# Gate tiles copied to SBUF before the tanh, up tiles multiplied by the copy, first uses of buffers that no longer wait for each other, and longer assumed latencies, in a fused attention and SwiGLU block

## The chip, the cores and the metric

The kernel runs on one core of a Trainium2 chip. The metric is device microseconds (us) of one execution, lower is better. Quoted times are medians of a kernel's runs; ratios are always against runs of the kernel before on the same chip. A span, read from a profile, is about 2 us shorter than the timed run.

Engines in the profile: PE is TensorE (matmuls), PEld its weight loads, DVE is VectorE, ACT is ScalarE, POOL is GpSimd, SPq is the queue that issues the DMA transfers.

## The reference, cut to what matters

Shapes: S = 2048 rows, D = 1024, H = 32 heads of 32, one shared key and value head, F = 3584.

```python
h = layernorm(x) * (1 + ca) + sa              # sa ... gb from silu(c) @ w_mod
x = x + ga * attention(h, wq, wk, wv, wo)     # softmax over 2048 keys, 32 query heads, 1 kv head
h = layernorm(x) * (1 + cb) + sb
x = x + gb * ((silu(h @ w1) * (h @ w3)) @ w2)
```

The 2048 rows are worked off in 8 blocks of 256: attention of a block, then output projection, layer norm and feed-forward of that block. Feed-forward is 672 matmuls of 128x128 by 256 columns a block, 5376 in all.

## The kernel before

All instructions are collected in a graph. A list scheduler then puts them, when the program is built, into one fixed order for each engine, with assumed durations and latencies. The built program holds a list for each engine, with semaphore waits where the graph demands them; in the profile of the kernel before, for one, the weight loads of the scores waited 180.5 us for exps. So an instruction's place is decided by the assumptions, and its time is what the profile shows.

```python
SEM_LAT = 0.06                                   # assumed semaphore latency, us
class Dag:
    def add(self, eng, fn, reads=(), writes=(), dur=0.1, lat=0.1, prio=5, ...):
        ...
        for k in reads:                          # a read waits for the last writer of the key
            ...
        for k in writes:                         # a write waits for the last writer and all readers,
            ...                                  # and becomes the last writer
    def schedule(self, banks):                   # greedy: next free engine takes its best ready node;
        ...                                      # a PSUM bank is free once all nodes of its group ended
def dve_t(n, rate=1):
    return n / rate / 960.0 + 0.08               # assumed time of a VectorE operation
```

The program uses eight PSUM banks: six (SP) belong to the attention scores as long as there are any, two (PB) serve everything else. The feed-forward loop, for a pair of gate and up tiles (128 x 512 each):

```python
for fp in range(NF // 2):                        # 14 pairs a block
    sl, rk = ring()                              # weight slot; rk: keys that the slot lies over
    for w, src in enumerate((w1_in, w3_in)):
        dma(..., ("ring", sl, w), writes=[("RW", sl, w)] + (rk if w == 0 else rk[1:]), ...)
    for w in range(2):
        g = mm_group(2 * NC, gmm, ...)           # 16 matmuls into one PSUM bank
        if w == 0:
            G.add("act", lambda e, g=g: e.activation(TS[:, 0:2 * qn], PB[g.bank][:, 0:2 * qn], ACT.Tanh, scale=0.5),
                  writes=["TS"] + alias("TS"), groups=[(g, "r")], ...)
            G.add("dve", lambda e, g=g: e.scalar_tensor_tensor(          # (tanh + 1) * gate
                TT[:, 0:2 * qn], TS[:, 0:2 * qn], 1.0, PB[g.bank][:, 0:2 * qn], ALU.add, ALU.mult),
                reads=["TS"], writes=["TT"] + alias("TT"), groups=[(g, "r")], ...)
        else:
            G.add("dve", lambda e, g=g, fp=fp: e.tensor_tensor(HHT[...], TT[...], PB[g.bank][...], ALU.mult),
                reads=["TT"], writes=[("HHT", 2 * fp), ("HHT", 2 * fp + 1)] + alias(("HHT", fp)), ...)
```

`ring()` and `alias()` give, at the first use of a buffer, the keys of the older data under it. They are booked as writes, so each first use waits for the first use before it. At every use, first or not, `ring()` also gives a key RING of the slot, so that the first of a slot's two loads waits for the readers of both halves.

The softmax here doesn't subtract the row's maximum and nothing guards it: scores larger than these inputs give would overflow.

## Time and profile before

1299.79 us, median of 3 runs (1299.6 to 1301.11).

| stage of the profile (span 1298.3 us) | length | TensorE busy | VectorE busy | ScalarE busy |
|---|---|---|---|---|
| 100 us to the last score matmul at 1049.5 us | 949.5 us | 861 | 794 | 928 |
| from there to the end (the tail) | 248.8 us | 242 | 95 | 28 |

First the page of the kernel before: busy time by engine, and the span in 40 slices, busy share in tenths.

```profile
PE 1169.6 (90%) x15761; PEld 764.7 (59%) x15809; DVE 968.8 (75%) x1363; ACT 1009.1 (78%) x1146; POOL 28.5 (2%) x51
...
PE   4688987789899889997999979999799999999998
...
DVE  7788889868987888789887888878988865244242
ACT  1499999999999999999999989999999941011010
```

ScalarE is at 9 until slice 32 and then nearly idle, TensorE goes on to the end: two stages, with different limits. The whole-span shares hide this. The tail is feed-forward work that did not fit under attention.

The windows by stretch, kernel before: start:end, length, then busy us and count of PE, PEld, DVE, ACT, POOL, granted clock, DMA share, GB/s.

```profile
100.00:1049.50 949.50, 861.35 (x12604) 517.43 (x12635) 794.18 (x1058) 928.19 (x1043) 17.30 (x24) 0.96 0.46 129
1049.50:1298.30 248.80, 241.83 (x2205) 210.12 (x2201) 95.41 (x159) 27.62 (x45) 3.15 (x8) 1.00 0.99 264
```

The waits from 100 to 1050 us, kernel before: who waited for whom, us in total, times, longest.

```profile
PEld SP L702 <- ACT UREG L712: 180.5, 443, 2.2
...
ACT UREG L712 <- PE PB L655: 10.6, 6, 2.9
ACT UREG L712 <- PE SP L702: 9.9, 13, 1.5
```

L702 are the score matmuls, L712 the exps, L655 the value matmuls. TensorE waits for exps (180.5 us); ScalarE, busy 928 of the 949.5 us, hardly waits (10.6 and 9.9 us). ScalarE sets the pace here. (A weight load of the scores can wait while TensorE still multiplies: TensorE was idle for 88 of the 949.5 us in all.)

Groups by line and shape, kernel before: count, then busy us and mean ns of one, then idle before.

```profile
L830 ACT ACTIVATE WREG<-PB 128x512 bf16<-128x512 f32 x84 | 60.6, 722 | 70.3 <-PE PB L824 70.3
L833 DVE SCALAR_TENSOR_TENSOR WREG<-WREG,PB 128x512 bf16<-128x512 bf16 x84 | 56.8, 676 | 28.8 <-ACT WREG L830 25.8
...
L837 DVE TENSOR_TENSOR HREG<-WREG,PB 128x512 bf16<-128x512 bf16 x77 | 52.1, 676 | 9.8 <-PE PB L824 9.2
...
L866 DVE TENSOR_TENSOR X<-X,WREG 128x512 bf16<-128x512 bf16 x32 | 13.2, 413 | 0.7
```

A tanh out of PSUM (0.722 us) and two VectorE operations of 0.676 us each make a pair's product; L866 shows what a two-operand operation took when all was bf16 in SBUF (0.413 us).

### The profile page before, as it was taken

The numbers are of one execution on the slowest core, as the hardware profiler recorded it, in microseconds if no ns is written. First come the engines' busy times: TensorE is split into PE (matmuls) and PEld (weight loads), VectorE is DVE, ScalarE is ACT, GpSimd is POOL, SyncE is SP. The second block draws the span as 40 slices with busy tenths as digits, with TensorE's granted clock in tenths as the row PEclk, the third lists the DMA queues.
The fourth block names the chain that finished last, engine by engine and source line by source line (L and its number), as shares of the span: only waits on it lengthen the run. The fifth ranks groups of instructions, "written<-read, shape, count | busy, mean of one in ns | idle before, by whom it ended". The sixth has DMA issues, their size and how long they took to land.

```text
span 1298.3 us, 35924 instructions
## 1 busy us (share of the span) xinstructions
PE 1169.6 (90%) x15761; PEld 764.7 (59%) x15809; DVE 968.8 (75%) x1363; ACT 1009.1 (78%) x1146; POOL 28.5 (2%) x51
## 2 busy tenths in 40 slices
PE   4688987789899889997999979999799999999998
PEld 3333333455466446663666646665466678878887
DVE  7788889868987888789887888878988865244242
ACT  1499999999999999999999989999999941011010
POOL 1000000000100000000000000000100000000000
PEclk9898998989999989998999989999899999999999
DMA  9533001645256325571465724557155589999997
GB/s 311 197 104 110 2 2 34 178 134 139 76 162 196 99 69 165 158 205 57 133 175 152 218 76 132 147 166 210 34 164 147 162 245 247 281 284 271 298 290 180
DMA packets 370555, 207.96 MB, mean 160 GB/s; under 512 B 8928, under 2 KB 362208, under 8 KB 370400
## 3 DMA queue, kind: packets, MB, share of 16 engines
q1 hardware_dynamic: 370400, 205.68, 56.5%
q8 instruction: 124, 2.03, 0.7%
q14 instruction: 31, 0.25, 0.1%
HBM read 201.46 MB, written 4.19 MB: 158 GB/s over the span
## 4 chain that ended last, share of the span: by engine, by line
ACT 42%; PE 38%; issue 8%; DVE 6%; DMA 4%; SPq 1%; POOL 0%; DVEq 0%; ACTq 0%
ACT UREG L712 40%; PE PB L824 8%; PE SP L824 7%; PE SP L854 5%; PE PB L854 5%; PE SP L702 4%; PE PB L655 4%; ACT WREG L830 2%; DMA X<-in_A_x_dram 1%; PE PB L556 1%; DVE UREG L731 1%; PE PB L801 1%; DMA WREG<-in_w_mod_dram 1%; DMA UREG<-in_w_mod_dram 1%; PE PB L753 1%
## 5 line engine op out<-in xcount | busy, mean ns | idle before, releaser
L712 ACT ACTIVATE UREG<-SP 128x1024 bf16<-128x1024 f32 x1024 | 960.7, 1188 | 41.6 <-PE SP L702 30.3
L731 DVE TENSOR_TENSOR UREG<-UREG 128x2048 bf16<-128x2048 bf16 x256 | 309.5, 1209 | 37.7 <-ACT UREG L712 36.8
L702 PE MATMUL SP<-QT,KT 32*128 32x256 bf16 x4096 | 210.5, 281 | 61.6 <-ACT UREG L712 48.3
L726 DVE TENSOR_TENSOR UREG<-UREG 128x2048 bf16<-128x2048 bf16 x128 | 156.1, 1219 | 55.9 <-ACT UREG L712 54.1
L702 PEld LDWEIGHTS SP<-QT,KT 32*128 32x128 bf16 x4096 | 61.4, 93 | 207.4 <-ACT UREG L712 188.0
L824 PE MATMUL PB<-QT,WREG 128*128 128x256 bf16 x1280 | 166.3, 276 | 5.4 <-DVE WREG L833 2.0
L655 PE MATMUL PB<-UREG,V 128*32 128x256 bf16 x4096 | 144.7, 285 | 7.7 <-DVE QT L517 1.6
L824 PEld LDWEIGHTS PB<-QT,WREG 128*128 128x128 bf16 x1280 | 116.5, 98 | 46.3 <-issue 30.9
L655 PEld LDWEIGHTS PB<-UREG,V 128*32 128x32 bf16 x4096 | 100.4, 100 | 46.1 <-issue 15.6
L764 DVE RECIPROCAL DSB<-DSB 128x128 f32<-128x128 f32 x128 | 119.5, 940 | 0.2
L824 PE MATMUL PB<-QT,HREG 128*128 128x256 bf16 x848 | 114.0, 280 | 4.2 <-DVE HREG L837 1.3
L830 ACT ACTIVATE WREG<-PB 128x512 bf16<-128x512 f32 x84 | 60.6, 722 | 70.3 <-PE PB L824 70.3
L830 ACT ACTIVATE WREG<-SP 128x512 bf16<-128x512 f32 x28 | 16.7, 597 | 121.3 <-PE SP L824 121.3
L824 PEld LDWEIGHTS PB<-QT,HREG 128*128 128x128 bf16 x848 | 78.4, 100 | 34.3 <-issue 23.2
L833 DVE SCALAR_TENSOR_TENSOR WREG<-WREG,PB 128x512 bf16<-128x512 bf16 x84 | 56.8, 676 | 28.8 <-ACT WREG L830 25.8
L854 PE MATMUL PB<-WREG,HREG 128*128 128x256 bf16 x588 | 75.1, 274 | 1.3 <-DVE HREG L837 1.3
L556 PE MATMUL PB<-HREG,WREG 128*128 128x512 bf16 x237 | 61.0, 380 | 4.2 <-issue 2.2
L854 PEld LDWEIGHTS PB<-WREG,HREG 128*128 128x128 bf16 x588 | 52.6, 98 | 19.6 <-issue 14.2
L837 DVE TENSOR_TENSOR HREG<-WREG,PB 128x512 bf16<-128x512 bf16 x77 | 52.1, 676 | 9.8 <-PE PB L824 9.2
L824 PE MATMUL SP<-QT,WREG 128*128 128x256 bf16 x512 | 59.0, 273 | 0.0
L824 PE MATMUL PB<-QT,X 128*128 128x256 bf16 x448 | 57.4, 273 | 1.7 <-ACT UREG L712 1.0
L801 PE MATMUL PB<-WO,QT 128*128 128x512 bf16 x195 | 50.7, 380 | 7.1 <-DMA X<-in_A_x_dram 3.5
(94 smaller groups left out, 1038.3 us busy)
## 6 DMA issues: line engine op xcount, KB each, us to landing
WREG<-in_B_w_dram SPq DMA_DIRECT2D x112, 512.0 KB, 5.1
HREG<-in_B_w_dram SPq DMA_DIRECT2D x74, 512.0 KB, 5.2
WREG<-in_B_w_dram SPq DMA_DIRECT2D x33, 896.0 KB, 5.8
X<-in_B_w_dram SPq DMA_DIRECT2D x38, 512.0 KB, 5.1
HREG<-in_B_w_dram SPq DMA_DIRECT2D x21, 896.0 KB, 5.1
X<-in_B_w_dram SPq DMA_DIRECT2D x10, 896.0 KB, 5.1
X<-in_A_x_dram SPq DMA_DIRECT2D x32, 256.0 KB, 5.0
WREG<-in_w_mod_dram SPq DMA_DIRECT2D x16, 512.0 KB, 5.0
```

The costliest lines, as they stand in the source:

```text
L556: g = mm_group(NC, lambda e, b, c: e.matmul(b, WQ[:, c, f * P:(f + 1) * P], HT[:, c, sl], start=c == 0, stop=c == NC - 1), lambda c: [("WQ ...
L655: r = e.matmul(PB[g.bank][32 * gg:32 * gg + 32, 0:qn], V[:, kt, :], U[:, pu, (gg * npk + j) * qn:(gg * npk + j + 1) * qn], start=n == 0 an ...
L702: r = e.matmul(SP[:, b, o:o + qn], KT[32 * gg:32 * gg + 32, kts[j] * P:(kts[j] + 1) * P], QT[32 * gg:32 * gg + 32, f, q0:q0 + qn], start=T ...
L712: G.add("act", lambda e, u=u, h0=h0, n=n, b0=b0, nb=nb: e.activation(U[:, u, h0 * W:(h0 + n) * W].rearrange("p (b w) -> p b w", b=nb), SP[ ...
L726: G.add("dve", lambda e, tr=tr, u=u, fu=first_u: e.tensor_tensor(TR[:, tr, 0:4 * W], U[:, fu, 0:4 * W], U[:, u, 0:4 * W], ALU.add), reads= ...
L731: G.add("dve", lambda e, tr=tr, u=u: e.tensor_tensor(TR[:, tr, 0:4 * W], TR[:, tr, 0:4 * W], U[:, u, 0:4 * W], ALU.add), reads=[("TR", tr) ...
L764: G.add("dve", lambda e, h=h: e.reciprocal(DSB[:, h * 128:(h + 1) * 128], DSB[:, h * 128:(h + 1) * 128]), reads=["DSB"], writes=[("DSBr", ...
L801: g = mm_group(NC, lambda e, b, f, t=t, h=h: e.matmul(b, QT[:, f, t * P:(t + 1) * P], WO[:, f, h * 512:(h + 1) * 512], start=f == 0, stop= ...
L824: return e.matmul(b[:, j * qn:(j + 1) * qn], w13[:, w, c, j * P:(j + 1) * P], QT[:, c, q0:q0 + qn], start=c == 0, stop=c == NC - 1)
L830: G.add("act", lambda e, g=g: e.activation(TS[:, 0:2 * qn], PB[g.bank][:, 0:2 * qn], ACT.Tanh, scale=0.5), writes=["TS"] + alias("TS"), gr ...
L833: G.add("dve", lambda e, g=g: e.scalar_tensor_tensor(TT[:, 0:2 * qn], TS[:, 0:2 * qn], 1.0, PB[g.bank][:, 0:2 * qn], ALU.add, ALU.mult), r ...
L854: G.add("pe", lambda e, g=g, j=j, fc=fc, hf=hf, first=first, w2s=w2s: e.matmul(PB[g.bank][:, j * 256:(j + 1) * 256], HHT[:, hf * NH + fc, ...
```

## The change

Its intent: free the gate's PSUM bank by a VectorE copy instead of after a tanh that the order places behind exps; multiply the up tile by that copy at once, so its bank does not wait for the tanh either; let the first use of a buffer wait for the writer and the readers of what lay there without being booked as a writer itself, so that first uses no longer wait for each other; and assume longer latencies of ScalarE and VectorE results.

```diff
     def add(self, eng, fn, reads=(), writes=(), ...,
-            acq=None, groups=(), seq=None, dkey=None, nbytes=0, sbanks=(), after=()):
+            acq=None, groups=(), seq=None, dkey=None, nbytes=0, sbanks=(), after=(), clear=()):
         n = Node()
+        lat = {"act": 0.25, "dve": 0.15}.get(eng, lat)
 ...
+        for k in clear:
+            for r in [self.last_write.get(k)] + self.readers.get(k, []):
+                if r is not None:
+                    deps[id(r)] = r
 ...  # weight loads
-                    ("ring", sl, w), writes=[("RW", sl, w)] + (rk if w == 0 else rk[1:]), nbytes=D * 512)
+                    ("ring", sl, w), writes=[("RW", sl, w)], nbytes=D * 512, clear=rk)
 ...  # gate
-                    G.add("act", ... activation(TS, PB[g.bank], ACT.Tanh, scale=0.5),
-                          writes=["TS"] + alias("TS"), groups=[(g, "r")], ...)
-                    G.add("dve", ... scalar_tensor_tensor(TT, TS, 1.0, PB[g.bank], ALU.add, ALU.mult), ...)
+                    G.add("dve", ... tensor_copy(GS[b], PB[g.bank][:, 0:2 * qn]),
+                          writes=[("GS", b)], clear=alias("GS") if b == NG - 1 else (), groups=[(g, "r")], ...)
+                    G.add("act", ... activation(TB[b], GS[b], ACT.Tanh, scale=0.5), reads=[("GS", b)], ...)
 ...  # up
-                    G.add("dve", ... tensor_tensor(HHT, TT, PB[g.bank], ALU.mult),
-                        writes=[...] + alias(("HHT", fp)), ...)
+                    G.add("dve", ... tensor_tensor(HHT, GS[b], PB[g.bank], ALU.mult),
+                        reads=[("GS", b)], writes=[...], clear=alias(("HHT", fp)), groups=[(g, "r")], ...)
+                    G.add("dve", ... scalar_tensor_tensor(HHT, TB[b], 1.0, HHT, ALU.add, ALU.mult), prio=2)
```

Cut: the down-projection loads and the small output tile get `clear=` the same way, the key RING is gone, two attention buffers (ASB and DSB) shrink to make room, and there are two copy buffers.

More of the change, by code (lines that the diff above doesn't have):

```diff
@@ L351, in build @@
     GBB = sb("GBB", [P, D], BF16)
+    NG = 2
+    TP = -1
+    GSB = sb("GSB", [P, (NG - 1) * 1024], BF16)
+    GS = [GSB[:, i * 1024:i * 1024 + 512] for i in range(NG - 1)] + [WREG[:, 3 * 4096:3 * 4096 + 512]]
+    TB = [GSB[:, i * 1024 + 512:i * 1024 + 1024] for i in range(NG - 1)] + [WREG[:, 3 * 4096 + 512:3 * 4096 + 1024]]
     XN = sb("XN", [P, 4, D], BF16)
-    ASB = sb("ASB", [P, 512], F32)
-    DSB = sb("DSB", [P, 512], F32)
+    ASB = sb("ASB", [P, QB], F32)
+    DSB = sb("DSB", [P, QB], F32)
     WKR = sb("WKR", [P, NC, 4, 32], BF16)
@@ L408, in build, with dma @@
           reads=["IDENT"], writes=["IDENT"], dur=0.4)
-    def dma(fn, key, reads=(), writes=(), nbytes=0, after=()):
-        return G.add("sp", fn, reads=reads, writes=writes, dur=0.06, dkey=key, nbytes=nbytes, after=after)
+    def dma(fn, key, reads=(), writes=(), nbytes=0, after=(), clear=()):
+        return G.add("sp", fn, reads=reads, writes=writes, dur=0.06, dkey=key, nbytes=nbytes, after=after, clear=clear)
     dma(lambda e: e.dma_start(CROW[:], c_in.rearrange("o (k p) -> (o k) p", p=P)), "c", writes=["CROW"], nbytes=2048)
@@ L772, in build @@
     ring_n = [0]
+    WKEYS = [("WMS", i) for i in range(3)] + WQK + [("WQ", 0), ("WQ", 1)]
     ring_first = set()
@@ L778, in ring @@
         ring_n[0] += 1
-        keys = [("RING", sl)]
+        keys = []
         if sl not in ring_first:
@@ L782, in ring @@
             if sl < 3:
-                keys += [("WMS", i) for i in range(3)] + WQK + [("WQ", 0), ("WQ", 1)]
+                keys = WKEYS
             elif sl < 5:
-                keys += [HKEY]
+                keys = [HKEY]
             else:
-                keys += [("X", i) for i in range(4, 8)]
+                keys = [("X", i) for i in range(4, 8)]
         return sl, keys
@@ L825, in gmm @@
                                     start=c == 0, stop=c == NC - 1)
-                g = mm_group(2 * NC, gmm, lambda i, w=w, sl=sl: [("RING", sl), ("RW", sl, w)] + qkeys(i % NC, q0, qn),
+                g = mm_group(2 * NC, gmm, lambda i, w=w, sl=sl: [("RW", sl, w)] + qkeys(i % NC, q0, qn),
                              n_cols=qn, late=NC)
                 gs.append(g)
+                b = fp % NG
                 if w == 0:
-                    G.add("act", lambda e, g=g: e.activation(TS[:, 0:2 * qn], PB[g.bank][:, 0:2 * qn], ACT.Tanh,
-                                                             scale=0.5),
-                          writes=["TS"] + alias("TS"), groups=[(g, "r")], dur=act_t(2 * qn), prio=-1)
-                    G.add("dve", lambda e, g=g: e.scalar_tensor_tensor(
-                        TT[:, 0:2 * qn], TS[:, 0:2 * qn], 1.0, PB[g.bank][:, 0:2 * qn], ALU.add, ALU.mult),
-                        reads=["TS"], writes=["TT"] + alias("TT"), groups=[(g, "r")], dur=dve_t(2 * qn), prio=0)
-                else:
-                    G.add("dve", lambda e, g=g, fp=fp: e.tensor_tensor(
-                        HHT[:, 2 * fp:2 * fp + 2, 0:qn], TT[:, 0:2 * qn].rearrange("p (j q) -> p j q", j=2),
@@ new lines, in post @@
+                    G.add("dve", lambda e, g=g, b=b: e.tensor_copy(GS[b], PB[g.bank][:, 0:2 * qn]),
+                          writes=[("GS", b)], clear=alias("GS") if b == NG - 1 else (), groups=[(g, "r")], dur=dve_t(2 * qn), prio=0)
+                    G.add("act", lambda e, b=b: e.activation(TB[b], GS[b], ACT.Tanh, scale=0.5),
+                          reads=[("GS", b)], writes=[("TB", b)], clear=alias("TB") if b == NG - 1 else (), dur=act_t(2 * qn), prio=TP)
+                else:
+                    G.add("dve", lambda e, g=g, fp=fp, b=b: e.tensor_tensor(
+                        HHT[:, 2 * fp:2 * fp + 2, 0:qn], GS[b].rearrange("p (j q) -> p j q", j=2),
@@ L839, in post @@
                         PB[g.bank][:, 0:2 * qn].rearrange("p (j q) -> p j q", j=2), ALU.mult),
-                        reads=["TT"], writes=[("HHT", 2 * fp), ("HHT", 2 * fp + 1)] + alias(("HHT", fp)),
+                        reads=[("GS", b)], writes=[("HHT", 2 * fp), ("HHT", 2 * fp + 1)], clear=alias(("HHT", fp)),
                         groups=[(g, "r")], dur=dve_t(2 * qn), prio=0)
+                    G.add("dve", lambda e, fp=fp, b=b: e.scalar_tensor_tensor(
+                        HHT[:, 2 * fp:2 * fp + 2, 0:qn], TB[b].rearrange("p (j q) -> p j q", j=2), 1.0,
+                        HHT[:, 2 * fp:2 * fp + 2, 0:qn], ALU.add, ALU.mult),
+                        reads=[("TB", b), ("HHT", 2 * fp), ("HHT", 2 * fp + 1)],
+                        writes=[("HHT", 2 * fp), ("HHT", 2 * fp + 1)], dur=dve_t(2 * qn), prio=2)
@@ L849, in post @@
                     w2s, w2_in[hf * NH * P:(hf + 1) * NH * P, q * 256:(q + 1) * 256].rearrange("(c p) f -> p c f", p=P)),
-                    ("ring", sl, 0), writes=[("RW", sl, 0), ("RW", sl, 1)] + rk, nbytes=NH * P * 512)
+                    ("ring", sl, 0), writes=[("RW", sl, 0), ("RW", sl, 1)], nbytes=NH * P * 512, clear=rk)
                 for fc in range(NH):
@@ L856, in post @@
                             w2s[:, fc, :], start=first, stop=hf == 1 and fc == NH - 1, skip_group_check=True),
-                            reads=[("RING", sl), ("RW", sl, 0), ("RW", sl, 1), ("HHT", hf * NH + fc)], dur=256 / 2400.0 + 0.0026, lat=0.2,
+                            reads=[("RW", sl, 0), ("RW", sl, 1), ("HHT", hf * NH + fc)], dur=256 / 2400.0 + 0.0026, lat=0.2,
                             acq=g if first else None, groups=[(g, "w")], mode="F")
@@ L862, in post @@
                 GBB[:, q * 256:(q + 1) * 256].unsqueeze(1).broadcast_to([P, nt, 256]), ALU.mult),
-                reads=[("GBB", q // 2)], writes=[("O2B", ob)] + alias(("O2B", ob)), groups=[(g, "r")],
+                reads=[("GBB", q // 2)], writes=[("O2B", ob)], clear=alias(("O2B", ob)), groups=[(g, "r")],
                 dur=dve_t(nt * 256), prio=1)
@@ L885, in alias @@
             return [HKEY]
-        return [("WMS", i) for i in range(3)] + WQK + [("WQ", 0), ("WQ", 1)]
+        return WKEYS
     for bi, (q0, qn) in enumerate(BLOCKS):
```

## The prediction

> **What bounds the kernel now.** Two stages (windows by stretch). Until the last score matmul at 1049.5 us ScalarE sets the pace: busy 929 of the 950 us from 100 to 1050, with exps about 0.92 us apart and 70 tanhs of about 0.5 us each beside them. TensorE waits 180 us there for exps before score weight loads (table of waits); VectorE is busy 809 of 950 us (85%). After 1049.5 us only feed-forward work is left: TensorE is busy 242 of 249 us, a 128x256 matmul every 109 ns (16 in 1.75 us in the chain of waits). So the time is: end of the exps + the feed-forward matmuls that did not fit under them.
>
> **What the change does**, per pair of gate and up tiles:
> - ScalarE: still one tanh, now from a bf16 SBUF copy. [...]
> - VectorE: before, two PSUM ops of 0.676 us; after, copy and multiply from PSUM (0.68 each, as other such ops) and one three-operand op wholly in SBUF. [...] Net +0.7 us a pair.
> - PSUM: the gate bank is freed by the copy instead of after a tanh queued behind exps plus another VectorE op. Two banks serve feed-forward, value and output matmuls under attention, so this is the real gain.
> - Weight loads wait for less. TensorE waits under 4 us for them in all: worth nothing.
> - The static schedule is recomputed, with longer assumed latencies. The order of instructions shows 1647 feed-forward matmuls behind the last score matmul (before 2057), and 32 output-projection matmuls (before 64).
>
> **Sum.** Tail: 1647 x 0.1092 = 180, projection 32 x 0.216 = 7, rest and final store 8, stalls 2: 197 us instead of 249; 52 us gained, all critical. Attention gets longer: 82 tanhs under it instead of 70, +6; [...]heavier lumps between score matmuls (one about 9 us, two near 4.8; before none over 3.7), +8 of ScalarE idling. VectorE is the risk: 82 x 2.04 - 70 x 1.35 = +73 us and about +9 for two more row tiles raise it from 85% to some 93% of attention, in program order; late copies hold PSUM banks, then TensorE, then ScalarE: 0 to 30 us.
>
> 1298.3 - 52 + 6[...] + 8 = 1263; congestion puts mass above, earlier bank release that closes some of ScalarE's 21 us of idling puts mass below. **Prediction 1263 us, 1244 to 1292 in 8 of 10.** Faster by over 2% 0.69, within 2% 0.26, slower 0.05.
>
> **What would show it.** Last exp at 1055 to 1080 us; tail of 193 to 202 us with TensorE over 95% busy; VectorE 91 to 95% busy from 100 us to the last exp; TensorE's wait for exps some 40 us below 180; three feed-forward groups on VectorE at 0.67 to 0.69 us each; tanh mean within 0.1 us of before. Wrong steps would show as ScalarE waiting for matmuls well over 21 us (VectorE congestion reaching it), or DMA waits in the tail, which already moves 250 to 290 GB/s.
>
> **What would make it wrong.** VectorE over its capacity where gate and up tiles are dense, so that the last exp slides 40 us or more[...].

The marked cuts took out what no run or trace had shown: a cost of the tanh's new source, and the reason for taking the third VectorE operation at 0.68 us, like the PSUM operations. That 0.68 us was an assumption. In the trace of the kernel before, the only all-SBUF bf16 operation on two tensors of that size, L866, took 0.413 us, and the forecast named that time for the third operation as a case that would make it wrong, with 1250 us or less (its estimate). The sum came to 1263 us; the term for dearer tanhs is cut from it, and the terms left, 1298.3 - 52 + 6 + 8, come to 1260 us.

## More of the kernel before

The timeline of the DMA queue, 205 to 262 us, kernel before: start, us from first to last issue, what, count.

```profile
205.69 48.66 SPq L817 DMA_DIRECT2D WREG<-in_B_w_dram  x11
254.39 6.80 SPq L817 DMA_DIRECT2D HREG<-in_B_w_dram  x2
```

These are the first feed-forward weights; one more load went out just before the window. Eleven loads took 48.7 us to be issued.

## The result, and the profile after

1260.86 us, median of 4 runs (1258.97 to 1262.16), against 1300.45 us before. The ratio is 0.969 (95% interval 0.9668 to 0.9712). Ratios here are the mean time of one kernel's fast runs over that of the other's fast runs of the same rounds, so not quite the ratio of the quoted medians. Line numbers move: 702 becomes 712, 712 becomes 722, 655 becomes 665, 824 becomes 835.

The page after: busy time and slices.

```profile
PE 1161.1 (92%) x15762; PEld 760.2 (60%) x15809; DVE 1026.9 (82%) x1475; ACT 1011.3 (80%) x1146; POOL 32.0 (3%) x51
...
PE   4589998999999989998999899998999899999998
...
DVE  7888888998989998899988998789988899365352
ACT  1499999999999999999999989998999998011010
```

The windows after, cut at its own last score matmul (1062.7 us):

```profile
100.00:1062.70 962.70, 904.65 (x13025) 556.03 (x13059) 856.10 (x1181) 936.02 (x1054) 22.38 (x28) 0.98 0.50 141
1062.70:1258.60 195.90, 190.28 (x1781) 166.93 (x1775) 91.48 (x148) 21.97 (x34) 1.58 (x4) 1.00 1.00 263
```

The tail shrank by 52.9 us (248.8 to 195.9) and attention grew by 13.2 us, which makes the 39.7 us between the spans. ScalarE is busy 7.8 us more in attention, with 11 more tanhs under it, and idle 5.4 us more (26.7 us against 21.3). TensorE's granted clock is 1.00 in both tails, so the shorter tail is not due to it; in attention it is 0.96 before and 0.98 after, and no run shows whether that is a cause or a result.

The waits from 100 to 1060 us, after:

```profile
PEld SP L712 <- ACT UREG L722: 158.1, 437, 1.7
...
ACT UREG L722 <- PE PB L665: 10.4, 7, 4.3
...
ACT UREG L722 <- PE SP L712: 7.7, 10, 1.4
```

TensorE waits 22 us less at the score weight loads.

Groups in the same stretch, after. The tanh (L844) now reads a copy; VectorE has three operations instead of two, each as dear as the old ones.

```profile
L842 DVE CAST GSB<-PB 128x512 bf16<-128x512 f32 x41 | 27.6, 674 | 1.5 <-PE PB L835 1.3
L847 DVE TENSOR_TENSOR HREG<-GSB,PB 128x512 bf16<-128x512 bf16 x40 | 27.1, 678 | 1.9 <-PE PB L835 1.7
L852 DVE SCALAR_TENSOR_TENSOR HREG<-GSB,HREG 128x512 bf16<-128x512 bf16 x40 | 27.1, 678 | 0.4
```

In the tail, where the exps are over, the mean of a tanh can be compared: 0.597 us before and 0.630 us after. Before, 1060 to 1298 us, out of PSUM:

```profile
L830 ACT ACTIVATE WREG<-SP 128x512 bf16<-128x512 f32 x27 | 16.1, 597 | 115.7 <-PE SP L824 115.7
```

After, 1070 to 1258 us, out of SBUF:

```profile
L844 ACT ACTIVATE WREG<-WREG 128x512 bf16<-128x512 bf16 x15 | 9.4, 630 | 52.4 <-DVE WREG L842 52.4
```

Out of the copy a tanh took 0.033 us longer here.

The DMA queue's timeline after, 205 to 262 us:

```profile
204.81 8.00 SPq L828 DMA_DIRECT2D WREG<-in_B_w_dram  x5
212.85 7.11 SPq L828 DMA_DIRECT2D HREG<-in_B_w_dram  x4
220.06 14.36 SPq L828 DMA_DIRECT2D WREG<-in_B_w_dram  x6
237.71 10.56 SPq L828 DMA_DIRECT2D HREG<-in_B_w_dram  x4
```

In this window nineteen loads went out by 248.3 us, nine of them in the first 15 us; before, thirteen by 261.2 us.

So the time was as predicted. Whether the stated reasons were right, the two profiles alone don't tell, because the change has three parts. The experiments take it apart.

### The profile page after: what moved, and what is told of

Read it like the earlier page. It is cut to its first block, busy times and chain, and to the rows that moved or that the text cites. A ratio compares the mean times of both kernels' runs of the same rounds, so it can differ in the third digit from the quotient of the medians.

```text
span 1258.6 us, 36037 instructions
## 1 busy us (share of the span) xinstructions
PE 1161.1 (92%) x15762; PEld 760.2 (60%) x15809; DVE 1026.9 (82%) x1475; ACT 1011.3 (80%) x1146; POOL 32.0 (3%) x51
## 4 chain that ended last, share of the span: by engine, by line
ACT 46%; PE 31%; issue 10%; DVE 9%; DMA 3%; SPq 1%; POOL 1%; DVEq 0%; ACTq 0%
ACT UREG L722 43%; PE PB L835 8%; PE SP L835 6%; PE SP L869 4%; PE PB L869 4%; PE SP L712 3%; DVE UREG L741 2%; PE PB L665 2%; ACT GSB L844 2%; ACT WREG L844 1%; PE PB L812 1%; DMA WREG<-in_w_mod_dram 1%; PE PB L566 1%; DVE UREG L736 1%; DMA UREG<-in_w_mod_dram 1%
## 5 line engine op out<-in xcount | busy, mean ns | idle before, releaser
L835 PE MATMUL PB<-QT,WREG 128*128 128x256 bf16 x1440 | 182.1, 275 | 1.7 <-DVE GSB L842 0.6
L835 PEld LDWEIGHTS PB<-QT,WREG 128*128 128x128 bf16 x1440 | 131.8, 98 | 41.6 <-issue 27.1
L835 PE MATMUL PB<-QT,HREG 128*128 128x256 bf16 x944 | 124.3, 277 | 1.0 <-DVE QT L527 0.5
L844 ACT ACTIVATE GSB<-GSB 128x512 bf16<-128x512 bf16 x56 | 43.2, 771 | 96.4 <-DVE GSB L842 96.4
L869 PE MATMUL PB<-WREG,HREG 128*128 128x256 bf16 x728 | 91.7, 273 | 0.3 <-DVE DSB L771 0.2
L844 ACT ACTIVATE WREG<-WREG 128x512 bf16<-128x512 bf16 x56 | 42.4, 758 | 55.6 <-DVE WREG L842 55.6
L869 PEld LDWEIGHTS PB<-WREG,HREG 128*128 128x128 bf16 x728 | 66.4, 98 | 20.1 <-issue 13.1
L869 PE MATMUL PB<-HREG 128*128 128x256 bf16 x420 | 54.2, 273 | 0.6 <-DVE WREG L875 0.6
L835 PEld LDWEIGHTS PB<-QT,X 128*128 128x128 bf16 x448 | 42.2, 101 | 17.6 <-issue 11.6
L769 DVE TENSOR_TENSOR ASB<-ASB,PB 128x256 f32<-128x256 f32 x63 | 26.2, 416 | 25.4 <-PE PB L763 25.1
```

Of the source, the lines that this page charges most:

```text
L769: G.add("dve", lambda e, g=g: e.tensor_tensor(ASB[:, 0:qn], ASB[:, 0:qn], PB[g.bank][:, 0:qn], ALU.add), reads=["ASB"], writes=["ASB"], gr ...
L835: return e.matmul(b[:, j * qn:(j + 1) * qn], w13[:, w, c, j * P:(j + 1) * P], QT[:, c, q0:q0 + qn], start=c == 0, stop=c == NC - 1)
L844: G.add("act", lambda e, b=b: e.activation(TB[b], GS[b], ACT.Tanh, scale=0.5), reads=[("GS", b)], writes=[("TB", b)], clear=alias("TB") if ...
L869: G.add("pe", lambda e, g=g, j=j, fc=fc, hf=hf, first=first, w2s=w2s: e.matmul(PB[g.bank][:, j * 256:(j + 1) * 256], HHT[:, hf * NH + fc, ...
```

## The experiments

Theory as predicted: the gain is the earlier release of PSUM banks by the gate rewrite; VectorE's extra work costs some of it; the waiting rule of the loads is worth nothing. Rivals: (a) the waiting rule or the assumed latencies make the gain; (b) any new order of the greedy scheduler might have.

A tool for all of them: the number of feed-forward matmuls placed behind the last score matmul is read from the built program. Call it N. In every profile below

tail = 10 us + 0.1092 us x N + 0.216 us x (output-projection matmuls behind the last score matmul)

holds within 2 us in most profiles and within 5.2 us in the worst (b_clear). The 0.1092 and 0.216 us are read from the kernel before's tail (16 feed-forward matmuls in 1.75 us, 16 projection matmuls in 3.45 us), and the 10 us are the remainder in the first two profiles. The projection matmuls behind the last score are 64 in before and b_lat, 50 in b_clearlat, 32 in all others. What remains is when the last score matmul comes.

All runs, with the profile's split. The last score and the tail are those of the one profiled execution, whose time can differ from the median (by 5.6 us in a_hold, 2.7 us in b_clearlat, less in the others). "Early" is the number of feed-forward matmuls from 200 to 300 us, counted by their weight loads; where it is empty it was not counted. The rule is the new waiting of first uses and loads, the latencies are 0.25 and 0.15 us, the gate is the rewrite of the tanh path, and "other" marks runs in which further assumptions of the scheduler were moved.

| run | gate | rule | latencies | N | early | last score, us | tail, us | time, us | ratio to before |
|---|---|---|---|---|---|---|---|---|---|
| before | | | | 2057 | 252 | 1049.5 | 248.8 | 1299 to 1301 | 1 |
| b_lat | | | yes | 2075 | 263 | 1044.2 | 251.6 | 1297.5 | 0.9986 |
| b_clear | | yes | | 1968 | 397 | 1048.3 | 237.0 | 1287.1 | 0.991 |
| b_clearlat | | yes | yes | 1945 | 398 | 1039.1 | 235.0 | 1278.9 | 0.9842 |
| a_gate | yes | | | 1928 | 267 | 1064.3 | 230.8 | 1294.9 | 0.997 |
| a_nolat | yes | yes | | 1814 | 410 | 1051.5 | 214.9 | 1270.6 | 0.9773 |
| after | yes | yes | yes | 1647 | 431 | 1062.7 | 195.9 | 1260.9 | 0.969 |
| a_noclear | yes | loads not | yes | 1647 | 416 | 1065.1 | 195.9 | 1264.7 | 0.9728 |
| a_hold | bank held | yes | yes | 1936 | 384 | 1061.1 | 230.4 | 1299.2 | 0.9984 |
| a_uplate | up late | yes | yes | 1895 | 405 | 1059.2 | 223.6 | 1286.1 | 0.9889 |
| a_rec8 | yes | yes | yes | 1647 | | 1061.6 | 195.8 | 1259.7 | 0.9701 |
| a_cal | yes | yes | other | 1403 | 463 | 1080.6 | 169.5 | 1253.4 | 0.9643 |
| a_cal_rec8 | yes | yes | other | 1403 | | 1081.2 | 170.0 | 1253.6 | 0.9653 |
| a_best | yes | yes | other | 820 | 504 | 1100.3 | 106.7 | 1208.8 | 0.9307 |

### First four: the side parts, the two banks, the loads

b_clearlat has the old tanh path (bank freed after tanh and product) in the changed kernel. a_hold adds one thing:

```diff
 G.add("act", lambda e, b=b: e.activation(TB[b], GS[b], ACT.Tanh, scale=0.5),
-      reads=[("GS", b)], writes=[("TB", b)], ...)
+      reads=[("GS", b)], writes=[("TB", b)], groups=[(g, "r")], ...)   # bank free only after the tanh
```

a_uplate swaps the last two operations:

```diff
-HHT = GS[b] * PB[up bank];  HHT = (TB[b] + 1) * HHT
+TB[b] = (TB[b] + 1) * GS[b];  HHT = TB[b] * PB[up bank]
```

a_noclear books the weight loads as before, but not the first uses of the small tiles and of the product buffer HHT:

```diff
-("ring", sl, w), writes=[("RW", sl, w)], nbytes=D * 512, clear=rk)
+("ring", sl, w), writes=[("RW", sl, w)] + (rk if w == 0 else rk[1:]), nbytes=D * 512)
```

Expected of b_clearlat:

> The kernel before with the two side parts of the change only: longer assumed latencies in the static schedule, and first weight loads that wait for readers alone; gate and up tiles leave PSUM as before. Its order has 1945 feed-forward and 50 projection matmuls behind the last score matmul (before 2057 and 64, after 1647 and 32). My theory (the gate rewrite frees PSUM banks earlier, and that lets more work be placed under the exps): tail about 233 us, so 1280 to 1292 us, a small part of the gain. Rival (the gain comes from the new assumed latencies and waiting rules): 1258 to 1270 us.

Measured: 1278.9 us, ratio 0.9842 (0.9816 to 0.9868). A miss: I had put it down as a small part of the gain, and it is half. The tail was 235 us where 233 were expected, but attention was 10 us shorter than before (in the profiled execution, the fastest of the four).

> The changed kernel with the same instructions, but the gate bank counts as free only after the tanh, as before, although the copy has read it long ago. 1936 feed-forward matmuls behind the last score matmul (after 1647). My theory: tail about 228 us, time 1283 to 1294 us, most of the gain gone. Rival (the gain is not the gate bank's early release but cheaper reads or the side parts): 1258 to 1268 us.

Measured: 1299.2 us, ratio 0.9984 (0.9954 to 1.0014). All of the gain is gone, the side parts' too. The windows of a_hold:

```profile
100.00:1061.10 961.10, 880.58 (x12743) 533.68 (x12739) 839.20 (x1144) 929.73 (x1045) 20.67 (x26) 0.97 0.47 133
1061.10:1291.50 230.40, 224.04 (x2080) 195.97 (x2072) 112.73 (x183) 27.06 (x42) 3.26 (x6) 0.99 0.97 258
```

Its instructions are those of the changed kernel. What differs is when a bank counts as free, and hence the order: 289 feed-forward matmuls more behind the last score. So here the copy gives nothing unless its early release is used (0.9984 against 0.969). Against b_clearlat, which has a late release too and no copy, N is the same (1936 and 1945) and the last score comes 22 us later; ScalarE's busy time differs by 2 us (929.7 and 927.9), so it is idle time of ScalarE (31.4 us against 11.2).

> The changed kernel with the last two VectorE operations of a pair swapped: (tanh + 1) times the gate copy first, all in SBUF, then times the up tile out of PSUM, so the up bank waits for the tanh again while the gate bank is still freed by the copy. Same number and kind of operations. 1895 feed-forward matmuls behind the last score matmul. If the up bank's release matters as much as the gate bank's: 1279 to 1291 us. If the gate bank alone is the gain, as my prediction put it: 1258 to 1268 us.

Measured: 1286.1 us, ratio 0.9889 (0.9869 to 0.991). The up bank's early release matters too, some two thirds as much as the gate bank's. My prediction had named only the gate bank.

> The changed kernel with the old waiting rules of the weight loads. The order on every compute engine is identical to the changed kernel's; only the DMA queue's order and waits differ. My theory: no effect, 1257 to 1265 us. Rival (weights that arrive earlier help): 1275 us or more.

Measured: 1264.7 us, ratio 0.9728 (0.9705 to 0.9751), 0.4% over the changed kernel's 0.969, with the same order on all compute engines. The DMA queue's timeline of a_noclear, 205 to 262 us:

```profile
204.91 0.58 SPq L828 DMA_DIRECT2D HREG<-in_B_w_dram  x1
209.98 0.37 SPq L828 DMA_DIRECT2D WREG<-in_B_w_dram  x1
211.44 0.37 SPq L828 DMA_DIRECT2D HREG<-in_B_w_dram  x1
213.87 0.37 SPq L828 DMA_DIRECT2D WREG<-in_B_w_dram  x1
...
223.54 15.05 SPq L828 DMA_DIRECT2D WREG<-in_B_w_dram  x8
246.06 6.05 SPq L828 DMA_DIRECT2D HREG<-in_B_w_dram  x4
```

The single lines at the start are loads into two regions that alternate. Nineteen loads were out by 252.1 us, against 248.3 us in the changed kernel and thirteen by 261.2 us in the kernel before. So this run does not bring the old slow loading back: what is left of the rule, at the first uses of the tiles, suffices for most of it. Given that, the loads' own old waits cost about 4 us, and even this is not clear of noise, as the two intervals overlap slightly.

### Next four: one part alone, and one assumption moved

b_lat is the kernel before with `lat = {"act": 0.25, "dve": 0.15}.get(eng, lat)` added. b_clear is b_clearlat without that line. a_nolat is the changed kernel without it. a_cal changes one number of the scheduler's assumptions:

```diff
 def dve_t(n, rate=1):
-    return n / rate / 960.0 + 0.08
+    return n / rate / 960.0 + 0.13
```

> The kernel before with the longer assumed latencies alone. 2075 feed-forward and 64 projection matmuls behind the last score matmul. The runs so far fit: tail = 10 us + 0.1092 us per feed-forward matmul + 0.216 us per projection matmul behind the last score matmul (within 2 us), so the tail should be 250 us. The two side parts together moved the last score matmul from 1049.5 to 1039.1 us. If the assumed latencies did that: last score matmul near 1040, time 1288 to 1295 us. If the waiting rule did it: near 1050, time 1298 to 1304 us.

Measured: 1297.5 us, ratio 0.9986 (0.9957 to 1.0015), last score at 1044.2 us. Alone the latencies are worth nothing that the runs can show.

> The kernel before with the new waiting rule of the weight loads alone. 1968 feed-forward and 32 projection matmuls behind the last score matmul: tail 232 us. If the waiting rule moved the last score matmul: near 1040, time 1270 to 1277 us. If the assumed latencies did: near 1050, time 1280 to 1287 us. If my prediction was right that the rule is worth nothing: 1297 to 1303 us.

Measured: 1287.1 us, ratio 0.991 (0.9878 to 0.9941), last score at 1048.3 us, tail 237 us where 232 were counted. The waiting rule alone gains 0.9%. "Worth nothing" in my prediction is refuted. The windows of the gate and up matmuls alone, 200 to 300 us (PE busy and count, PEld busy and count, granted clock, DMA share, GB/s), of the kernel before:

```profile
200.00:300.00 100.00, 37.20 (x252) 24.69 (x252) 0.88 0.46 125
```

and of b_clear:

```profile
200.00:300.00 100.00, 51.61 (x396) 35.90 (x397) 0.93 0.61 171
```

By the weight loads (397 against 252), the rule lets 145 more matmuls run in the first 100 us of feed-forward. Not all of them are taken out of the tail: N fell by 89 (2057 to 1968), and the tail by 11.8 us.

> The changed kernel with the old, shorter assumed latencies. 1814 feed-forward and 32 projection matmuls behind the last score matmul: tail 215 us. If the last score matmul stays near 1063 us: 1275 to 1284 us. If the longer latencies also save ScalarE waits: last score matmul at 1068 or later, 1284 to 1292 us. If they are worth nothing: 1258 to 1266 us.

Measured: 1270.6 us, ratio 0.9773 (0.9749 to 0.9797). Below the range: the tail was the 215 us counted, but the last score came at 1051.5 us, 11 us earlier than in the changed kernel. So with less work placed under the scores, attention was shorter. Against a_nolat the changed kernel has 19.0 us less tail and 11.2 us more attention: more than half of what is moved out of the tail comes back.

> The changed kernel with one number of the static schedule's assumptions nearer to the trace: the fixed part of a VectorE operation 0.13 us, not 0.08 (512 elements out of PSUM: 0.663 us assumed, 0.68 measured). 1403 feed-forward and 32 projection matmuls behind the last score matmul: tail 170 us. If the last score matmul stays at 1060 to 1075 us: 1231 to 1247 us, faster than both kernels. If VectorE is the limit in attention, the matmuls that are placed there push the last exp out to 1085 us or more, and the time is 1255 us or more.

Measured: 1253.4 us, ratio 0.9643 (0.9619 to 0.9667). Between the two: it beats both kernels, but of 26.4 us taken from the tail 17.9 us came back in attention.

### Last four: the gate alone, VectorE's weight, and how far the order goes

a_gate is the changed kernel with the latencies and all waiting rules as before. a_rec8 and a_cal_rec8 keep the exact order of the changed kernel and of a_cal, and make each of 128 reciprocals small; their results are wrong:

```diff
-e.reciprocal(DSB[:, h * 128:(h + 1) * 128], DSB[:, h * 128:(h + 1) * 128])
+e.reciprocal(DSB[:, h * 128:h * 128 + 8], DSB[:, h * 128:h * 128 + 8])
```

a_best moves three assumptions of the scheduler. It was chosen because it had the smallest N of 18 combinations built (820 to 1800):

```diff
-SEM_LAT = 0.06
+SEM_LAT = 0.07
-        lat = {"act": 0.25, "dve": 0.15}.get(eng, lat)
+        lat = {"act": 0.30, "dve": 0.15}.get(eng, lat)
-    return n / rate / 960.0 + 0.08
+    return n / rate / 960.0 + 0.13
```

> The gate rewrite alone: copy, tanh from SBUF, up tile times the copy; old assumed latencies and old waiting rules everywhere (also for the first writes of the small tiles that lie over the old weights). 1928 feed-forward and 32 projection matmuls behind the last score matmul: tail 227 us. If the rewrite is worth what it adds on top of the new waiting rule (1287.1 to 1270.6 us, 16 us): 1281 to 1289 us. If it needs the new rule to pay (its order alone gains only 129 matmuls, and VectorE has more to do): last score matmul at 1058 or later, 1284 to 1296 us. My prediction, that the early bank release is the real gain and the rule worth nothing: 1256 to 1270 us.

Measured: 1294.9 us, ratio 0.997 (0.9943 to 0.9998), last score at 1064.3 us. The gate rewrite alone gains next to nothing. Its early count is 267, as without the change. With the rule in place the same rewrite takes the ratio from 0.991 to 0.9773 (b_clear to a_nolat). So the two parts gain more together (2.3%) than the sum of what each gains alone (0.9% and 0.3%).

> The changed kernel in its exact order on every engine, but each reciprocal takes 8 columns instead of 128: some 0.75 us less each on VectorE, 128 times, about 95 us in all; results are wrong on purpose. If VectorE, busy 89% of the attention stage, delays ScalarE there (0 to 30 us in my prediction): last score matmul 5 to 20 us earlier than 1062.7, time 1240 to 1256 us. If it delays nothing: 1258 to 1263 us.

Measured: 1259.7 us, ratio 0.9701 (0.9679 to 0.9724): the changed kernel's time. The reciprocals of the changed kernel:

```profile
L774 DVE RECIPROCAL DSB<-DSB 128x128 f32<-128x128 f32 x128 | 119.4, 939 | 0.4
```

and the reciprocals and the windows of a_rec8:

```profile
L774 DVE RECIPROCAL DSB<-DSB 128x8 f32<-128x8 f32 x128 | 23.7, 192 | 0.4
```

```profile
100.00:1061.60 961.60, 903.26 (x13018) 555.14 (x13057) 777.96 (x1181) 935.53 (x1054) 23.28 (x28) 0.98 0.50 141
```

VectorE's busy time in attention fell from 856 to 778 us (89% to 81%), and the last score matmul moved by 1.1 us. So these 78 us of VectorE's load do not delay this order. That it has room at 89% says nothing of an order that packs more onto it.

> The same short reciprocals (wrong on purpose) in the order of the run with the recalibrated VectorE time, whose last score matmul came 18 us later than the changed kernel's (1080.6 against 1062.7). If VectorE causes that: last score matmul at 1070 or earlier, 1235 to 1244 us. If the lumps of other work between the score matmuls in the order itself cause it: 1250 to 1255 us.

Measured: 1253.6 us, ratio 0.9653 (0.963 to 0.9676), last score at 1081.2 us against 1080.6. The longer attention of a_cal does not come from this part of VectorE's load either.

> The changed kernel with three of the static schedule's assumptions moved: fixed part of a VectorE operation 0.13 us (0.08), ScalarE latency 0.30 us (0.25), semaphore latency 0.07 us (0.06). The program is otherwise the same, and only the order differs: 820 feed-forward matmuls behind the last score matmul (1647), tail about 107 us, and 88 us more TensorE work under the scores. If ScalarE still set the pace there, the last score matmul would come at 1065 to 1085 us, and the time would be 1173 to 1195 us. I expect TensorE to become the limit, so that half to three quarters of the work shifted comes back as a longer attention stage: last score matmul near 1115 to 1135, time 1222 to 1245 us. If moving work under the scores no longer pays at all: 1250 us or more.

Measured: 1208.8 us, ratio 0.9307 (0.928 to 0.9333), correct. It beats both kernels and my range. The windows of a_best:

```profile
100.00:1100.30 1000.30, 966.28 (x13785) 631.69 (x13824) 894.93 (x1242) 949.93 (x1070) 24.14 (x28) 0.99 0.57 163
1100.30:1207.00 106.70, 100.29 (x954) 85.99 (x952) 51.12 (x85) 11.10 (x17) 1.58 (x4) 0.99 0.84 222
```

and its waits from 100 to 1100.3 us:

```profile
PEld SP L712 <- ACT UREG L722: 88.6, 298, 1.7
...
ACT UREG L722 <- PE PB L665: 43.2, 27, 3.5
```

TensorE's wait for exps is down from 158 to 89 us, and ScalarE waits 43 us for value matmuls where it waited 10: the pace begins to pass from ScalarE (busy 95% of the stage, 97% in the changed kernel) to TensorE (97%, against 94%). Against the changed kernel the tail lost 89.2 us and attention gained 37.6 us.

### How much is luck of the order

The scheduler is greedy, and N jumps with small changes of its assumptions. I built, but did not time, twelve variants each (VectorE's fixed part 0.09 to 0.15 us, semaphore latency 0.05 to 0.08 us). N lay between 1960 and 2139 for the kernel before, and between 1403 and 1893 for the changed one (1403 is a_cal). With the five semaphore latencies alone, a_hold gave 1772 to 1931, a_uplate 1856 to 1936 and the changed kernel 1512 to 1704. So the change moves N well beyond its scatter, and so does each of the two early releases. But over those five N of the changed kernel itself ranges over 192 matmuls, which are 21 us of tail. Part of that would come back in attention, yet the size that I give to any one part from a single order is uncertain by some 10 us (an estimate: those 21 us, less the share that came back from a_nolat to the changed kernel, 11.2 of 19.0 us).

## Why the prediction was right, and where its reasons were not

- **Total, 1263 us (1244 to 1292), right.** The sum started from the span. The span after is 1258.6 us, the time 1260.9 us.
- **Tail 197 us, right: 195.9 us**, TensorE busy 97% of it. This rested on N read from the built order, and on 109 ns a matmul (16 in 1.75 us). That is why the total holds although the causes were mixed up: the count already contained all three parts.
- **Attention +17 us with the cut term (+14 without it), nearly right: +13.2 us.** ScalarE's busy time rose by 7.8 us (predicted 9 with the cut term, 6 without it), its idle time by 5.4 us (predicted 8).
- **"PSUM: ... so this is the real gain", half right.** The early release is needed: taking it from the gate bank cost 3.0% of the ratio (a_hold against after), from the up bank 2.0%. It is not sufficient: the rewrite without the rule is worth 0.3% (a_gate).
- **"Weight loads wait for less ... worth nothing", wrong; this step failed.** I judged the rule by TensorE's waits for DMA, under 4 us. But the wait stood on the DMA queue, and the scheduler, which knows the dependency, had placed the matmuls behind it later. The rule is worth 0.9% alone and lets 145 more matmuls run between 200 and 300 us. The kernel before: a wait of the DMA queue (200 to 265 us), a line of VectorE's timeline (200 to 256 us) and one of the queue's (222 to 232 us):

```profile
SPq L817 <- DVE WREG L833: 21.5, 1, 21.5
```

```profile
226.91 0.69 DVE L833 SCALAR_TENSOR_TENSOR WREG<-WREG,PB 128x512 bf16<-128x512 bf16 x1 [0.68 <-ACT WREG L830]
```

```profile
227.62 4.61 SPq L817 DMA_DIRECT2D WREG<-in_B_w_dram  x3
```

  After a load issued at 205.7 us the queue stood still for 21.5 us, until the first pair's product of tanh and gate (L833) was done, and the next load went out 0.02 us later. The load's slot and the product's tile both lie over the old weights and book the same keys, so load, first use and next load form a chain. In the changed kernel this wait is absent, and the first five loads of the window shown above are out by 212.8 us. Which half of the rule counts, the loads or the first uses of the tiles, is open. With the loads' old waits back (a_noclear) the order of the compute engines does not change, the early count stays at 416 and the ratio rises by 0.4%. No run undid the first uses alone. Such programs were built, but not timed: with the first uses alone undone N rises from 1647 to 1732 in the changed kernel and does not change in b_clear and a_nolat; with both halves undone in the changed kernel it is 1904. So it seems, but is not timed, that breaking the chain at either half gives most of the gain.
- **Assumed latencies, only mentioned.** Alone nothing (b_lat); on top of the other two parts 0.8% (a_nolat to after), which is within what one order's luck can do.
- **VectorE +73 us as "the risk", 0 to 30 us: no cost found.** Three operations of 0.674 to 0.678 us each, as assumed: the third, all bf16 in SBUF, took 0.674 and 0.678 us, about as long as the old one out of PSUM (0.676 us); VectorE rose by 62 us to 89% (predicted 91 to 95%), and relieving it of 78 us moved the last score by 1.1 us (a_rec8). The 809 us (85%) from which I started were misread: the profile has 794 us (84%).
- **TensorE's wait for exps "some 40 us below 180": 22 us below.** The direction was right, the size too large.
- **Tanh out of the copy: 0.033 us dearer**, 0.630 us in the tail against 0.597.

## What to carry to other kernels

In a kernel whose engines run fixed lists, judge a dependency by what the order places early and late, and count that in the built program. TensorE's table of waits did not show the rule's worth here; the DMA queue's own, with its 21.5 us, pointed to it. Copying a tile out of PSUM paid here only where the order used the freed bank (ratio 0.969, against 0.9984 in a_hold), and for the most part only together with the freed dependencies of the first block (0.997 without them, in a_gate). And once a change has given the order more freedom, move the scheduler's assumptions: three constants were worth another 4% on the changed kernel (0.9307 against 0.969), more than the whole change. They are no substitute for it: in the twelve variants of the kernel before N never fell below 1960, and with the three constants of a_best it is 1968 (built, not timed).
